# Cross network (DCN), six layers: pairs of row blocks taken in turn on shared weight tiles, a second product split into seven

## Chip, cores and metric

One NeuronCore of a Trainium2 chip runs the kernel. The metric is device time in microseconds (us), as the median of repeated runs. TensorE multiplies, VectorE adds and multiplies element by element, ScalarE moves results out of PSUM, and the queue of SyncE (SP) issues nearly all DMAs.

## What is computed

```python
# x0: 16384 x 1024, ws: 6 x 1024 x 1024, bs: 6 x 1024, all bf16
x = x0
for l in range(6):
    proj = x @ ws[l] + bs[l]
    x = x0 * proj + x
return x
```

## The kernel before

**Tiles.** The 16384 rows are cut into 16 pairs of row blocks, 2 x 512 rows each (`NPAIR`, L36). A pair lies transposed in SBUF: feature on the partition, row on the free axis. `x0T` holds the inputs of a pair and `xst` the running x, each [128, 2 blocks, 8 feature chunks, 512 rows].

**Seven products for eight.** A layer of a pair is a 2 x 2 block product: two halves of the features in, two halves out, two row blocks. L326 to L439 compute it with seven products of 512 x 512 weights by 512 rows instead of eight (a Strassen scheme). The products are numbered: 1, 2 and 4 use plain quarters of the weights, 5, 6, 3 and 7 use sums and differences of quarters ("combos", `emit_combo`, L120), which are made during the first pair and saved to DRAM (`Lc`). On the other side they need differences of x: T1 to T4 (`Ops.t`, L153). One product is 4 output chunks `m` of 4 matmuls each (`mm`, L279), every matmul 128x128 weights by 128x512, so seven products are 112 matmuls.

**Product 2 is split once more.** From the second pair on (`small`, L260) product 2 is itself done by seven products of 256 x 256 weights by 256 rows (`inner`, L286, 4 matmuls of 128x256 each, 28 in place of 16 of 128x512). Its differences of x are `ti` (`inner_t`, L160, four VectorE instructions of 128x512), its weight combos are "product 8". Its parts go out through ScalarE to EA and EB (`evi`, L298) and are added by VectorE (L374, L376).

**Sums.** Products 1, 6, 7 and 4 add up in the four banks `pA` one after another, and ScalarE reads them out (`ev`, L292) after each: P1s, then U2s (1+6), U3s (1+6+7), and the output sum with 4. Products 5 and then 3 share the banks `pX`: P5s and S53. VectorE forms the four output quarters C1 and C2 from these, multiplies by `x0T` (`f_mul`, L311) and adds to x (`f_add`, L314).

**Order.** The loops are pair (L227), then layer (L257). A step is one layer of one pair; there are 96. A layer needs the whole layer before it, so the T differences for the next layer stand at the end of the step (L444 to L452) between the last sums. VectorE and ScalarE instructions are pinned to program order (`vtt`, `acopy`, `abias`). PSUM has two pools of four banks that change roles at each step (L263).

**Loads.** Weight tiles (512 KB) go through a ring of 12 (`wring`, L60) on the SP queue, about ten tiles ahead (`prefetch_upto`, L89, `PREF` L85), in the order of all_keys: every pair loads all eight tiles of every layer again. The x0 of the next pair comes by DMA transposes during layer 0 (L473 to L479) into one of two `x0T` tiles. A finished pair is transposed by DMA from `xst` into its own `x0T` tile, which serves as scratch, and two DMAs write that out (L483 to L488). The last pair is written out differently, in part by TensorE transposes (`out_pe`, L242).

Of the kernel before, what the change touches and what calls it, by code (L numbers as in the profile page):

```python
# [8 lines left out]
ADD = mybir.AluOpType.add  # L9
# [8 lines left out]
def kernel(  # L18
# [19 lines left out]

    pin = tc.keep_in_program_order

    def vtt(out, in0, in1, op):
        return pin(nc.vector.tensor_tensor(out=out, in0=in0, in1=in1, op=op))  # L42

# [6 lines left out]
    NQ = NB // 2  # L50
    HE = H // 2

    const = ctx.enter_context(tc.tile_pool(name="const", bufs=1))
    dram = ctx.enter_context(tc.tile_pool(name="dram", bufs=1, space=bass.MemoryType.DRAM))
    x0t_pool = ctx.enter_context(tc.tile_pool(name="x0t", bufs=2))
    xst_pool = ctx.enter_context(tc.tile_pool(name="xst", bufs=2))
    t_pool = ctx.enter_context(tc.tile_pool(name="tp", bufs=1))
    ev_pool = ctx.enter_context(tc.tile_pool(name="evp", bufs=7))
    cb_pool = ctx.enter_context(tc.tile_pool(name="cbp", bufs=2))
    wring = ctx.enter_context(tc.tile_pool(name="wring", bufs=12))  # L60
    ti_pool = ctx.enter_context(tc.tile_pool(name="tip", bufs=1))
    ei_pool = ctx.enter_context(tc.tile_pool(name="eip", bufs=1))
    ps = [ctx.enter_context(tc.tile_pool(name=f"ps{i}", bufs=KH, space=bass.MemoryType.PSUM)) for i in range(2)]
    stage_ctx = ExitStack()
    w12_pool = stage_ctx.enter_context(tc.tile_pool(name="w12", bufs=2))
    xo_pool = None

    Lc = dram.tile([L, 5, P, KH * H], BF16, name="Lc")
    CIDX = {5: 0, 6: 1, 7: 2, 3: 3, 8: 4}

    def w_src(l, pid):
        wl = ws[l]
        if pid == 1:
            return wl[0:H, 0:H].rearrange("(k p) e -> p k e", p=P)
        if pid == 2:
            return wl[H:D, 0:H].rearrange("(k p) e -> p k e", p=P)
        if pid == 4:
            return wl[H:D, H:D].rearrange("(k p) e -> p k e", p=P)
        return Lc[l, CIDX[pid]].rearrange("p (k e) -> p k e", k=KH)

    ORDER = [1, 2, 8, 5, 3, 6, 7, 4]
    all_keys = [(pr, l, pid) for pr in range(NPAIR) for l in range(L) for pid in ORDER if pr > 0 or pid != 8]
    key_pos = {k_: i for i, k_ in enumerate(all_keys)}
    is_dma = lambda k_: not (k_[0] == 0 and k_[2] in CIDX)
    PREF = 10  # L85
    wtiles = {}
    state = {"next": 0}

    def prefetch_upto(n):  # L89
        while state["next"] < min(n, len(all_keys)):  # L90
            k_ = all_keys[state["next"]]
            if is_dma(k_) and k_ not in wtiles:
                wt = wring.tile([P, KH, H], BF16, name="wp")
                state["last_dma"] = nc.sync.dma_start(wt[:], w_src(k_[1], k_[2]))
                wtiles[k_] = wt
            state["next"] += 1
# [6 lines left out]
    combo_st = {}  # L103
    pending_saves = []

    def flush_saves():
        for (l_, pid_, t_) in pending_saves:
            si = nc.sync.dma_start(Lc[l_, CIDX[pid_]].rearrange("p (k e) -> p k e", k=KH), t_[:])
            if state.get("last_dma") is not None:
                nosync(si, state["last_dma"], "combo save behind the urgent weight loads")  # L110
        pending_saves.clear()

    def load_w12(l):
        st = combo_st.setdefault(l, {})
        if "w12" not in st:
            st["w12"] = w12_pool.tile([P, KH, H], BF16, name="w12")
            state["last_dma"] = nc.sync.dma_start(st["w12"][:], ws[l][0:H, H:D].rearrange("(k p) e -> p k e", p=P))
        return st["w12"]

    def emit_combo(l, pid):  # L120
        prefetch_upto(key_pos[(0, l, 4)] + 1)
        W11, W21, W22 = wtiles[(0, l, 1)], wtiles[(0, l, 2)], wtiles[(0, l, 4)]
        w12 = load_w12(l)
        t_ = wring.tile([P, KH, H], BF16, name="wp")
        if pid == 5:
            vtt(t_[:], w12[:], W22[:], ADD)
        elif pid == 6:
            vtt(t_[:], wtiles[(0, l, 5)][:], W11[:], SUB)
        elif pid == 3:
            vtt(t_[:], W21[:], wtiles[(0, l, 6)][:], SUB)  # L130
        elif pid == 8:
            i11, i12 = W21[:, 0:2, 0:HE], W21[:, 0:2, HE:H]
            i21, i22 = W21[:, 2:4, 0:HE], W21[:, 2:4, HE:H]
            iv = t_[:].rearrange("p k (j e) -> p k j e", e=HE)
            vtt(iv[:, 0], i12, i22, ADD)
            vtt(iv[:, 3], i11, i12, SUB)
            vtt(iv[:, 1], iv[:, 0], i11, SUB)
            vtt(iv[:, 2], i21, iv[:, 1], SUB)
        else:
            vtt(t_[:], W11[:], w12[:], SUB)  # L140
        if pid != 8:
            wtiles[(0, l, pid)] = t_
        pending_saves.append((l, pid, t_))

    class Ops:
        def __init__(self, x, flip, small):
            b = lambda dh, r: x[:, r ^ flip, dh * KH:(dh + 1) * KH, :]
            self.B = {(dh, r): b(dh, r) for dh in range(2) for r in range(2)}
            self.T = {}
            self.small = small  # L150
            self.ti = None

        def t(self, i):  # L153
            B, T = self.B, self.T
            T[i] = t_pool.tile([P, KH, NB], BF16, name=f"T{i}")
            in0, in1 = {1: lambda: (B[0, 1], B[0, 0]), 2: lambda: (B[1, 1], T[1][:]),
                        3: lambda: (B[1, 1], B[0, 1]), 4: lambda: (B[1, 0], T[2][:])}[i]()
            vtt(T[i][:], in0, in1, SUB)

        def inner_t(self, which):  # L160
            if not self.small:
                return
            if self.ti is None:
                self.ti = ti_pool.tile([P, 4, 2, NQ], BF16, name="ti")
            ti, b = self.ti, self.B[1, 0]
            b11, b12 = b[:, 0:2, 0:NQ], b[:, 0:2, NQ:NB]
            b21, b22 = b[:, 2:4, 0:NQ], b[:, 2:4, NQ:NB]
            for i in which:
                in0, in1 = {1: (b12, b11), 2: (b22, ti[:, 0]), 3: (b22, b12), 4: (b21, ti[:, 1])}[i]
                vtt(ti[:, i - 1], in0, in1, SUB)  # L170

        def rhs(self, pid):
            B, T = self.B, self.T
            return {1: B[0, 0], 2: B[1, 0], 3: B[1, 1]}[pid] if pid <= 3 else T[{4: 4, 5: 1, 6: 2, 7: 3}[pid]][:]

    LK = L * KD
# [6 lines left out]
    x0T_next = x0t_pool.tile([P, 2, KD, NB], BF16, name="x0T")  # L183
    xrows = [ev_pool.tile([P, KH, NB], BF16, name="ev") for _ in range(2)]
    xrows += [t_pool.tile([P, KH, NB], BF16, name=f"T{i}") for i in (3, 4)]
    raw = {i: wring.tile([P, KH, H], BF16, name="wp") for i in (1, 2, 4)}
    combo_st[0] = {"w12": w12_pool.tile([P, KH, H], BF16, name="w12")}
# [5 lines left out]
    pin(nc.scalar.dma_start(raw[1][:], w_src(0, 1)))  # L193
    pin(nc.scalar.dma_start(raw[2][:], w_src(0, 2)))
    pin(nc.scalar.dma_start(combo_st[0]["w12"][:], ws[0][0:H, H:D].rearrange("(k p) e -> p k e", p=P)))
    pin(nc.scalar.dma_start(raw[4][:], w_src(0, 4)))
    for i in raw:
        wtiles[(0, 0, i)] = raw[i]
    warm_in = const.tile([P, 1], BF16, name="warm_in")
    acopy(warm_in[:], zero[:, 0:1])  # L200
    warm = ps[1].tile([P, NB], FP32, name="px")
# [3 lines left out]
    def transpose_rows(q):  # L205
        n, h = q // 2, q % 2
        for k in range(KH):
            pt = ps[1].tile([P, NB], FP32, name="px")
            for r in range(KH):
                nc.tensor.matmul(pt[:, r * P:(r + 1) * P], lhsT=xrows[q][:, r, k * P:(k + 1) * P], rhs=ident[:],  # L210
                                 start=(r == 0), stop=True, skip_group_check=True)
            dst = x0T_next[:, n, h * KH + k, :]
            if k % 2 == 0:
                acopy(dst, pt[:])
            else:
                pin(nc.vector.tensor_copy(out=dst, in_=pt[:]))  # L216

    transpose_rows(0)
    pb = ps[1].tile([P, NB], FP32, name="px")
    nc.tensor.matmul(pb[:, 0:LK], lhsT=b_rows[:], rhs=ident[0:LK, 0:LK], start=True, stop=True)  # L220
    pin(nc.vector.tensor_copy(out=b_all[:], in_=pb[:, 0:LK]))
    prefetch_upto(7)
    ops = Ops(x0T_next, 0, False)
    prefetch_upto(PREF)

    step = 0
    for pr in range(NPAIR):  # L227
        x0T = x0T_next
        xst = xst_pool.tile([P, 2, KD, NB], BF16, name="xst")
        last_pair = pr == NPAIR - 1  # L230
# [11 lines left out]
        def out_pe(pts, n, ms, src, start, yo):  # L242
            for j in range(KH):
# [3 lines left out]
                if yo is None:  # L247
                    continue
# [270 lines left out]
```

## Time and profile before

| | us |
|---|---|
| median of 3 runs (2316.15 to 2316.91) | 2316.63 |
| profiled execution: its own time | 2314.74 |
| profiled execution: span from the first to the last instruction | 2313.0 |
| TensorE busy | 2287.3 |
| VectorE busy | 1994.0 |
| ScalarE busy | 1832.8 |

Granted TensorE clock: 1.000 of full speed. In the profile, PE is TensorE matmul, PEld its weight load, DVE is VectorE, ACT is ScalarE, SPq is SyncE's queue. A busy time of PE counts pipelined matmuls by modelled ends, so that the start of one matmul to the start of the next says more than the length of one. L42 is the helper `vtt`, through which all VectorE sums go, so there tiles tell the instructions apart. The DVE timeline gives the length of an instruction, too; where instructions follow each other without an idle note in brackets, the distance between two starts is what one really costs. Some matmul records are missing from the trace, so counts in a group can be low.

### The profile page before, as it was taken

How to read it: one execution, taken by the hardware profiler on the slowest of the kernel's cores; microseconds unless marked ns; L12 is line 12 of the kernel's file. 1: busy time of each engine (PE TensorE's matmuls, PEld its weight loads, DVE VectorE, ACT ScalarE, POOL GpSimd, SP SyncE). 2: the span in 40 equal slices, each digit the busy share in tenths (PEclk: the TensorE clock that was granted, in tenths of full speed). 3: DMA queues.
4: the chain of work that ended last, by engine and by line, in shares of the span. 5: the costliest groups of instructions: out<-in, count | busy, mean ns of one | idle time of the engine just before them, and what ended most of it. 6: DMA issues, size and time to landing. Idle time of an engine off the chain costs nothing.

```text
span 2313.0 us, 31780 instructions
## 1 busy us (share of the span) xinstructions
PE 2287.3 (99%) x11723; PEld 1163.4 (50%) x11953; DVE 1994.0 (86%) x2233; ACT 1832.8 (79%) x2974; POOL 0.7 (0%) x6
## 2 busy tenths in 40 slices
PE   8999999999999999999999999999999999999998
PEld 4444555545455554555555454555545555554544
DVE  7998888888888888888888888888888888888887
ACT  6777878878787887878788787878878787887877
POOL 0000000000000000000000000000000000000000
PEclk9999999999999999999999999999999999999999
DMA  7769586695966959668596685967859578595763
GB/s 237 245 212 289 173 219 245 183 281 174 230 234 185 279 183 232 227 189 272 183 240 224 193 267 180 255 209 194 270 173 271 195 196 267 172 294 174 211 217 106
DMA packets 603548, 507.53 MB, mean 219 GB/s; under 512 B 387329, under 2 KB 541953, under 8 KB 603393
## 3 DMA queue, kind: packets, MB, share of 16 engines
q1 hardware_dynamic: 601280, 503.39, 72.1%
q10 hardware_dynamic: 2112, 2.10, 0.3%
q8 instruction: 95, 1.56, 0.3%
q14 instruction: 61, 0.49, 0.1%
HBM read 392.18 MB, written 49.28 MB: 191 GB/s over the span
## 4 chain that ended last, share of the span: by engine, by line
PE 92%; DVE 5%; issue 1%; DMA 0%; ACT 0%; DVEq 0%; ACTq 0%
PE px L283 80%; PE px L289 12%; DVE cb L42 2%; DVE wp L42 1%; DVE xst L42 1%; DVE T L42 1%; DMA ev<-in_x_dram 0%; ACT ev L45 0%; DMA wp<-in_ws_dram 0%; DMA Lc<-wp 0%; DVE x0T L216 0%; PE px L210 0%; DVE ti L42 0%; ACT cb L48 0%; ACT ev L48 0%
## 5 line engine op out<-in xcount | busy, mean ns | idle before, releaser
L283 PEld LDWEIGHTS <-wp 128*128 128x128 bf16 x9312 | 909.7, 98 | 1010.3 <-issue 7.1
L283 PE MATMUL px<-T,wp 128*128 128x512 bf16 x5992 | 1393.2, 379 | 10.2 <-DVE wp L42 2.1
L48 ACT ACTIVATE ev<-px,b_all 128x512 bf16<-128x512 f32 x1152 | 791.6, 687 | 224.2 <-PE px L283 216.2
L283 PE MATMUL px<-xst,wp 128*128 128x512 bf16 x2575 | 615.1, 379 | 6.5 <-DVE xst L42 3.1
L45 ACT CAST ev<-px 128x512 bf16<-128x512 f32 x798 | 466.5, 585 | 179.5 <-PE px L283 166.3
L42 DVE TENSOR_TENSOR cb<-cb,x0T 128x2048 bf16<-128x2048 bf16 (+1 forms) x386 | 469.8, 1218 | 9.9
L42 DVE TENSOR_TENSOR cb<-ev 128x1024 bf16<-128x1024 bf16 (+1 forms) x390 | 263.0, 696 | 231.4 <-ACT ev L45 231.4
L42 DVE TENSOR_TENSOR xst<-cb,xst 128x2048 bf16<-128x2048 bf16 x319 | 390.8, 1225 | 23.1 <-DVE cb L42 0.9
L48 ACT ACTIVATE cb<-px,b_all 128x512 bf16<-128x512 f32 x384 | 263.8, 687 | 67.7 <-PE px L283 55.6
L289 PEld LDWEIGHTS <-wp 128*128 128x128 bf16 x2520 | 246.0, 98 | 127.1
L289 PE MATMUL px<-ti,wp 128*128 128x256 bf16 x1440 | 215.8, 272 | 0.0
L45 ACT CAST ea<-px 128x512 bf16<-128x512 f32 x360 | 211.8, 588 | 0.0
L42 DVE TENSOR_TENSOR T<-xst,T 128x2048 bf16<-128x2048 bf16 x160 | 195.5, 1222 | 9.0 <-PE px L289 0.9
L42 DVE TENSOR_TENSOR T<-xst 128x2048 bf16<-128x2048 bf16 x160 | 194.9, 1218 | 0.0
L45 ACT CAST eb<-px 128x512 bf16<-128x512 f32 x270 | 160.2, 593 | 0.0
L289 PE MATMUL px<-xst,wp 128*128 128x256 bf16 x900 | 135.0, 273 | 0.0
L283 PE MATMUL px<-x0T,wp 128*128 128x512 bf16 x515 | 122.8, 379 | 0.8
L42 DVE TENSOR_TENSOR ea<-ea,eb 128x1024 bf16<-128x1024 bf16 (+1 forms) x180 | 99.9, 555 | 20.4 <-ACT eb L45 20.4
L42 DVE TENSOR_TENSOR cb<-ev,ea 128x2048 bf16<-128x2048 bf16 x90 | 109.7, 1218 | 0.0
L42 DVE TENSOR_TENSOR xst<-cb,x0T 128x2048 bf16<-128x2048 bf16 x64 | 78.4, 1225 | 2.2
L42 DVE TENSOR_TENSOR ti<-xst 128x512 bf16<-128x512 bf16 x150 | 63.2, 422 | 3.6
L42 DVE TENSOR_TENSOR ti<-xst,ti 128x512 bf16<-128x512 bf16 x150 | 62.7, 418 | 0.0
(33 smaller groups left out, 201.1 us busy)
## 6 DMA issues: line engine op xcount, KB each, us to landing
wp<-Lc SPq DMA_DIRECT2D x450, 512.0 KB, 3.7
wp<-in_ws_dram SPq DMA_DIRECT2D x285, 512.0 KB, 4.3
out_dram<-x0T SPq DMA_DIRECT2D x30, 1024.0 KB, 10.0
Lc<-wp SPq DMA_DIRECT2D x30, 512.0 KB, 3.1
w<-in_ws_dram SPq DMA_DIRECT2D x5, 512.0 KB, 4.5
wp<-in_ws_dram ACTq DMA_DIRECT2D x3, 512.0 KB, 7.6
ev<-in_x_dram SPq DMA_DIRECT2D x2, 512.0 KB, 6.9
T<-in_x_dram SPq DMA_DIRECT2D x2, 512.0 KB, 10.3
```

The lines of the kernel that those rows point to most:

```text
L42: return pin(nc.vector.tensor_tensor(out=out, in0=in0, in1=in1, op=op))
L45: return pin(nc.scalar.copy(out=out, in_=in_))
L48: return pin(nc.scalar.activation(out=out, in_=in_, func=IDENT, bias=bias, scale=1.0))
L283: nc.tensor.matmul(pts[m][:], lhsT=wt[:, k, m * P:(m + 1) * P], rhs=rhs[:, k, :], start=(start and k == 0), stop=(k == KH - 1), **kw)
L289: nc.tensor.matmul(pt[:, m * NQ:(m + 1) * NQ], lhsT=w[:, k, m * P:(m + 1) * P], rhs=rhs[:, k, :], start=(start and m == 0 and k == 0), sto ...
```

## The change

The changed kernel runs two pairs, A and B, side by side: for each of 8 couples `s`, for each layer, first the step of A and then the step of B, with the same weight tiles. The weights are loaded once per couple and layer: 7 x 6 x 9 = 378 loads after the first couple, through a ring of 11. Nothing is prefetched in A's step but what is missing; in B's step each product requests the tile ten places further on.

Product 4 is split like product 2, in all steps of couples 1 to 7 but the very last (83 steps), with its own differences `ti4` and its own weight combos ("product 9"). Product 2 is split in all 84 steps of couples 1 to 7; the first couple (pairs 0 and 1, 12 steps) splits nothing, while in the kernel before pair 1 split product 2. Of product 4's seven parts four go out through ScalarE into e4 and e5, three add into `pA` directly.

What a step leaves over is done at the start of the next step, which belongs to the other pair (`trail`, `defer`): the last of the seven parts of product 4, two of its read-outs, and the four VectorE steps of C2 (sum, correction by e4 and e5, multiplication, addition). The T differences move to the start of the pair's own step. T1 and T3 become one VectorE instruction of 128x4096 (T13), and so do the multiplications and the additions of C2's two halves. The half sums of 128x1024 become whole ones of 128x2048.

A finished pair is stored in the other pair's step (`store_out`). There are three `x0T` tiles; B's x0 is loaded during A's layer 0, one step ahead of its use. At the end, the last pair is written out wholly through TensorE transposes, 80 matmuls in five groups with 16 read-outs (`rows_out`).

The core of the diff, the new lines only where the old ones are gone as a whole:

```diff
-    x0t_pool = ctx.enter_context(tc.tile_pool(name="x0t", bufs=2))
-    ev_pool = ctx.enter_context(tc.tile_pool(name="evp", bufs=7))
-    wring = ctx.enter_context(tc.tile_pool(name="wring", bufs=12))
+    x0t_pool, xst_pool = pool("x0t", 3), pool("xst", 2)
+    ev_pool, cb_pool, wring = pool("evp", 6), pool("cbp", 2), pool("wring", RING)
-    ORDER = [1, 2, 8, 5, 3, 6, 7, 4]
+    ORDER = [1, 2, 8, 5, 3, 6, 4, 9, 7]
+            if part is None:
+                vtt(self.t13[:], self.src[:, 1].rearrange("p (i k) b -> p i k b", i=2), self.src[:, :, 0:KH, :], SUB)
+    def trail(Y, prompt):
...
+        out = [lambda: vtt(C2[:, 1], Y.U3s[:], Y.P5s[:], ADD)]
+        if Y.E4 is not None:
+            def s4():
+                e = Y.E4
+                for i in range(2):
+                    vtt(e[:, 2 * i:2 * i + 2, NQ:NB], e[:, 2 * i:2 * i + 2, (1 - i) * NQ:(2 - i) * NQ], Y.e5[:], ADD)
+            out.append(s4)
+            out.append(lambda: vtt(C2[:, 0], C2[:, 0], Y.E4[:], ADD))
+        out.append(lambda: vtt(C2[:], C2[:], eh1(x0T), MULT))
+        out.append(lambda: vtt(eh1(dst), C2[:], eh1(src), ADD))
-    for pr in range(NPAIR):
-        for l in range(L):
+    for s in range(NPAIR // 2):
+        for l in range(L):
+            for side in ("A", "B"):
+                X, Y = cur[side], prev
+                in2, in4 = s > 0, s > 0 and not last
...
+                todo = trail(Y, False)
+                if not first:
+                    X.T13()
...
+                mm(1, w1, pA, 0, True)
+                if Y is not None and Y.defer is not None:
+                    Y.defer()
+                ev(P1s, pA, 0, 0)
+                prompt = Y is not None and Y.l == L - 1
...
+                    own = [X.T2, X.T4]
+                    if in4:
+                        own.append(lambda: setattr(X, "ti4", inner_t(X.T[4], "ti4")))
+                seq = todo + own if prompt else [f for pair in zip(todo + [None] * 9, own + [None] * 9) for f in pair if f is not None]
+                for f in seq:
+                    f()
+                if prompt:
+                    store_out(Y)
...
+                if need2 and not late:
+                    N.ti2 = inner_t(N.rhs(2), "ti2")
...
+                fin(C1, 0, 0)()
...
+                if in4:
+                    mm(6, w6, pA, 0, False)
+                    ev(U2s, pA, 0)
+                    inner(half(z1), wr4[0, 0], b4[0, 0], True)
+                    evi(e4[0, 0], z1)
+                    mm(6, w6, pA, 1, False)
+                    ev(U2s, pA, 1)
+                    inner(half(z5), wj[:, 0], t4[:, 0], True)
+                    evi(X.e5[:], z5)
+                    mm(6, w6, pA, 2, False)
+                    ev(U2s, pA, 2)
+                    inner(half(z1), wj[:, 1], t4[:, 1], False)
+                    evi(e4[0, 1], z1)
+                    mm(6, w6, pA, 3, False)
+                    ev(U2s, pA, 3)
+                    mm(7, w7, pA, 0, False)
+                    ev(U3s, pA, 0, 1)
+                    inner(half(z1), wj[:, 3], t4[:, 2], False)
+                    evi(e4[1, 0], z1)
+                    for m in range(1, KH):
+                        mm(7, w7, pA, m, False)
+                        ev(U3s, pA, m, 1)
+                    inner(col(0, 0), wr4[1, 0], b4[1, 0], False)
+                    inner(col(0, 1), wj[:, 2], b4[1, 1], False)
+                    for m in range(2):
+                        ev(C2[:, 0], pA, m, 1)
+                    def defer(pA=pA, C2=C2, wr4=wr4, t4=t4, ev=ev, inner=inner, col=col):
+                        inner(col(2, 0), wr4[1, 1], t4[:, 3], False)
+                        for m in range(2, KH):
+                            ev(C2[:, 0], pA, m, 1)
...
+                vtt(C1[:, 1], U2s[:], S53[:], ADD)
+                fin(C1, 0, 1)()
```

## Prediction

> **What bounds the kernel now.** I read the page's busy times first, then the chain of work that ended last, then the timelines of single engines in one steady step (700 to 724 us). The page:
>
> ```profile
> PE 2287.3 (99%) x11723; PEld 1163.4 (50%) x11953; DVE 1994.0 (86%) x2233; ACT 1832.8 (79%) x2974; POOL 0.7 (0%) x6
> PE 92%; DVE 5%; issue 1%; DMA 0%; ACT 0%; DVEq 0%; ACTq 0%
> ```
>
> TensorE is the bound; VectorE has some 3 us in 24 to spare; no DMA is on the chain. So time is won only by fewer matmul columns, and only while VectorE keeps up. Now TensorE's timeline, steady step:
>
> ```profile
> 713.18 1.03 PE L283 MATMUL px<-xst,wp 128*128 128x512 bf16 x4
> 714.04 0.60 PE L289 MATMUL px<-xst,wp 128*128 128x256 bf16 x4
> 714.48 1.03 PE L283 MATMUL px<-T,wp 128*128 128x512 bf16 x4
> 715.34 0.60 PE L289 MATMUL px<-ti,wp 128*128 128x256 bf16 x4
> 715.78 0.60 PE L289 MATMUL px<-xst,wp 128*128 128x256 bf16 x4
> 716.21 1.03 PE L283 MATMUL px<-T,wp 128*128 128x512 bf16 x4
> ```
>
> Compare starts: four wide matmuls (128x512) take 0.86 us, four narrow ones (128x256) 0.435. The longest pieces of the chain repeat every 118.99 us, five steps (338.23, 457.22): a step is 23.80 us. It has 24 groups of four wide and 7 of four narrow, so a wide group is (23.80 - 7 x 0.435)/24 = 0.865. VectorE's timeline of the same step:
>
> ```profile
> 711.01 1.22 DVE L42 TENSOR_TENSOR T<-xst 128x2048 bf16<-128x2048 bf16 x1
> 712.14 0.42 DVE L42 TENSOR_TENSOR ti<-xst,ti 128x512 bf16<-128x512 bf16 x1
> 712.48 0.42 DVE L42 TENSOR_TENSOR ti<-xst 128x512 bf16<-128x512 bf16 x1
> 712.81 0.42 DVE L42 TENSOR_TENSOR ti<-xst,ti 128x512 bf16<-128x512 bf16 x1
> 713.15 1.22 DVE L42 TENSOR_TENSOR cb<-cb,x0T 128x2048 bf16<-128x2048 bf16 x1
> 714.40 1.22 DVE L42 TENSOR_TENSOR xst<-cb,xst 128x2048 bf16<-128x2048 bf16 x1
> 715.73 1.23 DVE L42 TENSOR_TENSOR T<-xst,T 128x2048 bf16<-128x2048 bf16 x1
> ```
>
> Starts lie closer than durations: 128x2048 costs 1.135 us when the next instruction doesn't need its result (711.01 to 712.14), 1.25 to 1.33 when it does (713.15, 714.40), 128x512 costs 0.335. The same timeline gives 0.605 for 128x1024. In pair 0, where VectorE also makes the weight combos, its queue is full and the step is 24.69 us (its Lc saves start at 48.78, 73.47, 98.14); these prices add up to 24.6 there. I trust them.
>
> **TensorE.** A step with both splits has 20 wide and 14 narrow groups: 20 x 0.865 + 14 x 0.435 = 23.39 us, against 23.80: 0.41 less. Before, pairs 2 to 15 are 84 steps of 23.80 = 1999.2; after, 83 of 23.39 and the last of 23.80 = 1965.2: **-34.0**.
>
> **First couple.** Before, pair 1 starts at 161.8 us and ends six steps later at 304.6. After: 12 steps without a split, 28 wide groups = 24.22 each by TensorE. VectorE there needs some 21 us (a layer's combos now fall on two steps, and three pairs of instructions are merged), so TensorE sets 24.2. The first step ran from 6.91 to 37.45, with 2.2 of waiting for VectorE's combos, which now come earlier; say 35.5. But the second step belongs to B, whose T13 stands in VectorE's queue behind the combos of layer 1, and these need weights queued on SP behind four x0 transposes (about 5 us each to issue) and four saves. That puts the weights near 36 and T13's end near 46, while TensorE wants it at 35.5 + 2 x 3.46 = 42.4: 3 us of wait. 35.5 + 3 + 11 x 24.22 = 304.9: **0** (bounds -3, no wait, and +6).
>
> **VectorE, one steady step after.** The built program has 22 instructions a step. Three of 128x4096 (T13, C2's multiplication and addition), by extrapolation 1.135 + 2048 x (1.135 - 0.335)/1536 = 2.20 each, one with a dependent next: 6.75. Ten of 128x2048: four dependent at 1.25 to 1.29, six at 1.135: 11.8. EA + EB 0.605 + 0.43, e4's correction 0.67, ti2 and ti4 1.47 each (as the four combos at 48.67). Sum **23.2**. No row shows a 128x4096; two whole durations of 128x2048 would be 2.45, and the floor is the slope alone, 2.13. Without any dependency cost the sum is 22.3; with every instruction at its whole duration (1.22, 0.42, 0.69, 2.29) it is 24.4. I take 23.2, nearest to the rows and to pair 0. So VectorE has 0.2 us to spare in 23.39. Waits in it: C1's second sum needs U2s, whose last read-out I lay at 19.45 us (16 wide, 11 narrow groups, 0.8 for ScalarE); VectorE comes there at 19.2. T13 may start when product 7 of the step before has read the old one, 0.87 before that step ends. It ends near 2.0; product 5 reads it at 5.2 (4 wide and 4 narrow groups). So VectorE can be 3 us late before TensorE feels it. If VectorE needs over 23.39, the step follows it one for one: 84 us per us.
>
> A rule speaks against the change. The Trainium skill, page "VectorE: DVE Perf Modes", section "The DRAIN you can't avoid", has the next instruction start only when the pipe of the one before is empty. Then each would cost its duration, and by that the step would be about 24.4 and the kernel slower; the starts above, 1.13 apart at durations of 1.22, contradict it.
>
> **ScalarE.** Now 16 read-outs with bias, at 0.59 from start to start (714.24 to 714.83), and 19 without, at 0.48 (716.02 to 716.50): 18.6 of 23.4 us. It hides. Each narrow product finds its bank read out over 0.8 us before, but for product 2's, which now waits 0.03 (717.51 to 718.40) and will again: 0.
>
> **Loads.** Half the weight traffic goes, but the list of waits names no weight load before a steady matmul: 0. A's step issues hardly any load and B's step nine, as tiles come free, each at least 5 us before use.
>
> **Ends of couples.** SP's queue at the end of a pair before:
>
> ```profile
> 1310.48 10.55 SPq L484 DMA_TRANSPOSE x0T<-xst  x1
> 1321.13 1.00 SPq L94 DMA_DIRECT2D wp<-Lc  x2
> 1322.41 6.20 SPq L487 DMA_DIRECT2D out_dram<-x0T  x2
> 1328.71 5.08 SPq L94 DMA_DIRECT2D wp<-in_ws_dram  x2
> 1335.04 11.57 SPq L477 DMA_TRANSPOSE x0T<-in_x_dram  x2
> ```
>
> From the store's transpose to the x0 load is 24.6 us, and its second half lands some 13 us later (5.8 to issue the first, 7.4 to landing by the page). After, the store of A starts about 9.8 us into B's last step, so B's new x0 lands at 47 to 49 with four weight loads in the queue; B's first step starts at 46.8 and its T13 would start at about 48 and is needed at 52. Just in time; the product before it needs only the first half. Seven such places, 0 to 3 us each: **+3**. The new `xst` is first written 5 us after the old one's transpose has landed.
>
> **End.** Before, 8.8 us from the last product (2304.2) to the end. After, ten read-outs on ScalarE follow the last product instead of six, one after the other, about 7.4 us, then the last write (2.9 to landing, 1.3 to the end): 11.6. Also pair 14's store (24.5 us from its transpose to landed writes, begun 9.8 into the last step of 23.8) is still writing at +10.5, ahead of the last writes: 13.5. **+4.7** (2.8 to 7).
>
> **Sum.** 2313.0 - 34.0 + 0 + 3 + 4.7 = 2286.7 span. The profiled execution's own time is 1.7 above its span, and the median of the runs 1.9 above that: **2290**.
>
> **Rivals.**
> - VectorE slightly over (128x4096 at 2.3 to 2.4, or new dependency gaps): step 23.5 to 23.7, on average +0.2 x 84 = 17: 2307. For: the margin is 1%. Against: pair 0's sum fits to 0.1. Chance 0.17.
> - **Slower:** VectorE's instructions can't overlap as before, because nearly every one now waits for another engine or the one before, so each costs its whole duration: step 24.4, +1.05 x 84 = +88: 2378. It decides from 23.70 (26 us/84 over 23.39). For: the duration column; against: the starts. Chance 0.10, with its milder forms from 2321.
> - B's x0 comes late at the seven couple ends: another 5 us each would put T13 3 us too late, 7 x 3 = 21: 2311. For: SP's long issue times in a row; against: 4 us of reserve. Chance 0.07.
> - The change doesn't bring fewer columns at full pace: narrow products alternate with wide ones on two banks, and each of e4's three returns to bank z1 waits for ScalarE. Price half the gain, 0.2 x 84 = 17: 2307. Against: a wide group lies between. Chance 0.05.
>
> **How the numbers follow.** Likeliest, TensorE-bound at 23.4, 2290, own range 2281 to 2299: 0.61. Range 2280 to 2313: it takes in the milder rivals and the bounds of the start and end, and leaves out the slow one. Within 0.2% (4.6 us, about what a measurement can tell) is 2312 to 2321. Faster 0.84, same 0.05, slower 0.11.
>
> **What would show it.** Right: steady steps 23.4 apart, PE near 99%, DVE busy about 96% with a short wait for ScalarE before C1's second sum, 128x4096 starts 2.2 apart. Wrong: PE idle before product 5 or 6 put down to DVE (T13, T2), DVE without any idle time and steps over 23.5, PE idle before B's first layers put down to DMA, more than 15 us after the last wide product.

## The result, and the profile after

The changed kernel takes 2303.63 us (median of 4 runs, 2302.99 to 2307.08) against 2316.6 before on the same chip: ratio 0.9947, 95% interval 0.993 to 0.9964. It is faster, by 13 us where 26 were forecast. Its profiled execution took 2303.93 us, span 2302.1; the forecast span was 2286.7, so 15.4 us are missing there. (In the median 13.6 are missing, since it lies 0.3 us below the profiled execution's own time, where the forecast added 1.9.) The page's busy times and the shares of the chain, as shown of before:

```profile
PE 2259.3 (98%) x12658; PEld 1258.0 (55%) x12909; DVE 2186.7 (95%) x2328; ACT 1912.4 (83%) x3294; POOL 0.7 (0%) x6
PE 81%; DVE 7%; DMA 7%; SPq 2%; issue 1%; ACT 0%; DVEq 0%
```

VectorE is now nearly as busy as TensorE (86% before), and DMAs, which had 0% of the chain, and SP's queue, which did not appear in it, have 9%. Where the time lies is read from three landmarks of TensorE's timeline: the first matmul of A's first step of couple 1 (before: of pair 2's first step), the first transposing matmul after the last product, and the end (us):

| | first couple | couples 1 to 7 | end | span |
|---|---|---|---|---|
| before | 305.1 | 1999.1 | 8.8 | 2313.0 |
| predicted | 304.9 | 1968.2 | 13.5 | 2286.7 |
| after | 312.2 | 1972.0 | 17.8 | 2302.1 |

So 7.3 of the missing 15.4 us lie in the first couple, 3.8 in the couples, 4.3 at the end.

**The steady step is as forecast.** Three steps take 70.14 us (the chain's longest pieces stand at 368.24, 438.38 and 508.52): 23.38 each, forecast 23.39. Such a stretch in numbers (columns: window, its length, busy us and count of PE, PEld, DVE, ACT, POOL, granted clock, DMA share, GB/s):

```profile
368.24:438.38 70.14, 69.72 (x402) 39.92 (x408) 69.21 (x77) 60.00 (x105) 0.00 (x0) 1.00 0.41 107
```

VectorE's timeline where it lags behind TensorE and so runs at its own pace:

```profile
1017.82 2.29 DVE L46 TENSOR_TENSOR T<-xst 128x4096 bf16<-128x4096 bf16 x1
1020.02 1.22 DVE L46 TENSOR_TENSOR cb<-ev 128x2048 bf16<-128x2048 bf16 x1
...
1041.01 2.28 DVE L46 TENSOR_TENSOR T<-xst 128x4096 bf16<-128x4096 bf16 x1
```

T13 costs 2.20 from start to start, with a duration of 2.28, and one step of VectorE's work is 1041.01 - 1017.82 = 23.19 us. Both were forecast (2.20 and 23.2).

**The start.** TensorE, whose notes in brackets tell idle time and releaser, and SP's queue at the first step of B and the next step of A:

```profile
51.65 5.18 PE L295 MATMUL px<-T,eb 128*128 128x512 bf16 x16 [7.63 <-DVE T L46]
56.67 1.67 PE L295 MATMUL px<-x0T,wp 128*128 128x512 bf16 x7
```

```profile
6.35 19.53 SPq L198 DMA_TRANSPOSE x0T<-in_x_dram  x3
...
27.03 5.68 SPq L198 DMA_TRANSPOSE x0T<-in_x_dram  x1
...
34.85 2.72 SPq L112 DMA_DIRECT2D wp<-in_ws_dram  x3
```

Product 5 waits 7.63 us for its T, which stands in VectorE's queue behind the combos of layer 1, which wait for raw weights that SP issues from 33.9 us on. Before them stand four x0 transpositions, two of them for pair 2, whose x0 VectorE first reads at 297.29. After the pause the 16 matmuls of product 5 took 5.02 us (51.65 to 56.67) where a product takes 3.45. The stretches of the profile tell why (columns as above):

```profile
52.00:57.00 5.00, 5.00 (x18) 2.04 (x17) 5.00 (x4) 1.88 (x4) 0.00 (x0) 0.72 0.00 0
57.00:62.00 5.00, 5.00 (x25) 2.25 (x23) 4.93 (x5) 3.79 (x6) 0.00 (x0) 1.00 0.01 2
```

The granted clock is 0.72 over the 5 us after the pause and 1.00 after that. The Trainium skill, page "TensorE: Matmul & The Clock Gate", section "What's actually happening", says that an idle window of some 3.4 us halves the clock and a busy one of that length restores it. By that a pause costs about 1.7 us more (an estimate from that page); here it was 5.02 - 3.45 = 1.57, which agrees.

**A couple's end.** SP, VectorE and TensorE around the end of a couple, B's last step starting at 1132.81:

```profile
1143.88 9.63 SPq L250 DMA_TRANSPOSE x0T<-xst  x1
...
1168.07 11.70 SPq L198 DMA_TRANSPOSE x0T<-in_x_dram  x2
```

```profile
1141.56 2.29 DVE L46 TENSOR_TENSOR xst<-cb,xst 128x4096 bf16<-128x4096 bf16 x1
...
1183.43 2.29 DVE L46 TENSOR_TENSOR T<-x0T 128x4096 bf16<-128x4096 bf16 x1 [1.65 <-DMA x0T<-in_x_dram]
```

```profile
1185.78 1.04 PE L295 MATMUL px<-T,wp 128*128 128x512 bf16 x4 [0.84 <-DVE T L46]
```

A's rows are finished at 1143.85, 11.0 us into the step (forecast 9.8); SP needs 39.5 us from there to B's x0; T13 starts 50.6 us after B's last step began (forecast 48), and product 5 waits. At couple 1's end that step begins at 568.96 and the rows are ready at 578.75, 9.8 us into it as forecast; T13, with 2.02 us of waiting for x0, still starts only at 619.02, 50.1 us into it. The six ends between couple 1 and couple 7 cost 7.7 us together (1972.0 less the 1964.3 that e9 below takes without a wait); the seventh such place, where the first couple ends at 312, shows no wait.

**The end.** SP's last issues:

```profile
2270.93 9.67 SPq L250 DMA_TRANSPOSE x0T<-xst  x1
2283.35 5.00 SPq L254 DMA_DIRECT2D out_dram<-x0T  x2
2288.43 9.98 SPq L534 DMA_DIRECT2D out_dram<-ev  x8
```

The last product ends at 2284.26. Pair 14's output writes are issued around then, and the eight last writes stand behind them until 2298.4.

### The profile page after: what moved, and what is told of

Its sections match the earlier page's. It is cut to its first block, busy times and chain, and to the rows that moved or that the text cites. A ratio compares the mean times of both kernels' runs of the same rounds, so it can differ in the third digit from the quotient of the medians.

```text
span 2302.1 us, 33220 instructions
## 1 busy us (share of the span) xinstructions
PE 2259.3 (98%) x12658; PEld 1258.0 (55%) x12909; DVE 2186.7 (95%) x2328; ACT 1912.4 (83%) x3294; POOL 0.7 (0%) x6
## 4 chain that ended last, share of the span: by engine, by line
PE 81%; DVE 7%; DMA 7%; SPq 2%; issue 1%; ACT 0%; DVEq 0%
PE px L295 63%; PE px L301 18%; DMA x0T<-xst 3%; DVE cb L46 3%; DMA out_dram<-x0T 3%; SPq L198 2%; DVE T L46 2%; DMA x0T<-in_x_dram 2%; DVE xst L46 1%; DVE ti L46 1%; DMA wp<-in_ws_dram 0%; DVE ea L46 0%; PE px L527 0%; SPq L254 0%; DVE e L46 0%
## 5 line engine op out<-in xcount | busy, mean ns | idle before, releaser
L295 PEld LDWEIGHTS <-wp 128*128 128x128 bf16 x7888 | 771.2, 98 | 742.1 <-DVE T L46 6.5
L295 PE MATMUL px<-T,wp 128*128 128x512 bf16 x4499 | 1111.6, 379 | 11.4 <-DVE T L46 4.8
L301 PEld LDWEIGHTS <-wp 128*128 128x128 bf16 x4676 | 457.2, 98 | 250.2 <-DMA wp<-in_ws_dram 1.6
L46 DVE TENSOR_TENSOR cb<-cb,x0T 128x2048 bf16<-128x2048 bf16 (+2 forms) x291 | 454.4, 1562 | 4.6
L301 PE MATMUL px<-ti,wp 128*128 128x256 bf16 x2672 | 400.9, 273 | 0.0
L46 DVE TENSOR_TENSOR xst<-cb,xst 128x2048 bf16<-128x2048 bf16 (+1 forms) x240 | 378.2, 1576 | 9.2 <-PE px L527 0.5
L46 DVE TENSOR_TENSOR cb<-ev 128x2048 bf16<-128x2048 bf16 (+1 forms) x205 | 248.8, 1214 | 30.5 <-ACT ev L52 30.1
L52 ACT CAST e<-px 128x512 bf16<-128x512 f32 x332 | 195.3, 588 | 0.7 <-PE px L301 0.7
L46 DVE TENSOR_TENSOR T<-xst 128x4096 bf16<-128x4096 bf16 x80 | 182.7, 2284 | 0.0
L301 PE MATMUL px<-T,wp 128*128 128x256 bf16 x996 | 135.9, 273 | 0.7 <-DMA wp<-in_ws_dram 0.7
L46 DVE TENSOR_TENSOR cb<-ev,ea 128x2048 bf16<-128x2048 bf16 x84 | 102.9, 1225 | 11.1 <-ACT ev L55 2.6
L46 DVE TENSOR_TENSOR cb<-cb,e 128x2048 bf16<-128x2048 bf16 x83 | 101.2, 1220 | 1.3
```

Source lines behind the costliest of these rows:

```text
L52: return pin(nc.scalar.copy(out=out, in_=in_))
L295: nc.tensor.matmul(pts[m][:], lhsT=wt[:, k, m * P:(m + 1) * P], rhs=rhs[:, k, :], start=(start and k == 0), stop=(k == KH - 1), **kw)
L301: nc.tensor.matmul(dst(m), lhsT=w[:, k, m * P:(m + 1) * P], rhs=rhs[:, k, :], start=(start and m == 0 and k == 0), stop=(k == 1), skip_gro ...
```

## The experiments

Theory **Q**: the steps are as forecast, and the rest is lost in SP's queue, which sets the start, the couples' ends and the end. Rival **V**: VectorE's full queue makes these waits, whatever SP does. All times are us; the landmarks are those of the table above. "Time" is the median of the runs (of e3 and e6, one run).

| kernel | first couple | couples 1 to 7 | end | span | time |
|---|---|---|---|---|---|
| after | 312.2 | 1972.0 | 17.8 | 2302.1 | 2303.63 |
| e1_x0_behind_raw | 302.9 | 1973.4 | 17.6 | 2293.9 | 2294.12 |
| e2_store_halves | 315.1 | 1979.4 | 15.8 | 2310.3 | 2312.22 |
| e3_no_store_transpose | 320.5 | 1964.3 | 16.9 | 2301.7 | 2303.48 |
| e6_no_store14 | 313.6 | 1976.0 | 11.2 | 2300.8 | 2302.56 |
| e7_raw_lasthalf | 302.9 | 1972.5 | 16.5 | 2291.9 | 2293.72 |
| e8_outs_pool | 303.1 | 2136.5 | 16.7 | 2456.3 | 2459.95 |
| e4_no_split4 | 314.0 | 1997.2 | 13.8 | 2325.0 | 2328.36 |
| e5_dve_plus1 | 313.8 | 2000.3 | 19.4 | 2333.5 | 2337.51 |
| e5_dve_plus2 | 313.6 | 2035.6 | 19.3 | 2368.4 | 2371.46 |
| e9_raw_no_store_transpose | 304.3 | 1964.3 | 15.0 | 2283.6 | 2284.43 |
| e10_tail_writes_act | 303.9 | 1973.4 | 15.9 | 2293.1 | 2294.66 |
| e11_no_split4_last_layer | 304.3 | 1969.5 | 11.0 | 2284.8 | 2286.28 |

**e1: raw weights of layer 1 ahead of pair 2's x0.**

```diff
-            pin(eng.dma_start(t[:], raw_src(l, pid)))
+            ld = pin(eng.dma_start(t[:], raw_src(l, pid)))
+            if eng is nc.sync:
+                state["last_dma"] = ld
```

`load_x0` already holds its transpositions behind the DMA in `state["last_dma"]`; the edit sets it during the first couple, too.

> The x0 transposes of pair 2 (two, some 6 us of SP issue each) no longer stand among the first DMAs; they are queued behind the weight loads of layer 2. Theory Q (SP's queue): in the changed kernel the weights of layer 1 are issued at 33.9 to 37.6 us, because two x0 transposes of pair 2 stand before them; without these they go out at about 27, VectorE's combos for layer 1 start at about 33 instead of 41.6, T13 ends before TensorE asks for it at 43.9, and the 7.6 us wait in the second step falls below 1 us: 7 us less, about 2296.5. Theory V (VectorE's queue itself is too full there, 36 us of work in the first 60): the wait stays above 5 us and the time at 2303 to 2304.

Ratio to before 0.9911 (0.9897 to 0.9924). SP now issues the raw weights 9 us earlier, behind two transpositions instead of four:

```profile
25.17 1.18 SPq L112 DMA_DIRECT2D ea<-in_ws_dram  x1
26.41 2.67 SPq L112 DMA_DIRECT2D wp<-in_ws_dram  x3
```

The wait before product 5 is gone and the first couple ends 9.3 us sooner, 7.6 of waiting and 1.6 of lowered clock. SP's order alone did this: Q for the start.

**e2: every store's transposition in two halves.**

```diff
-        nc.sync.dma_start_transpose(out=xo, in_=Y.xst[:].rearrange("r n k b -> r (n k b)"))
+        for n in range(2):
+            nc.sync.dma_start_transpose(out=Y.x0T[:, n].rearrange("p k (j r) -> p (k j) r", r=P),
+                                        in_=Y.xst[:, n].rearrange("r k b -> r (k b)"))
```

> The store of a finished pair transposes its two row blocks by two DMAs instead of one, so that the first write can start while the second half is still in flight. Theory Q: the writes are issued when SP is done with the second transpose, some 2 us earlier than now; the x0 of B, which waits for them, lands 2 us earlier, and the waits at the six later ends of couples (7.7 us in all, 0.5 to 2.5 each) fall to 2 or less; the end after the last product falls from 17.8 to about 15.5. Together 7 to 8 us less: about 2296. Theory V (the ends of couples wait because VectorE, with 0.2 us to spare in a step, comes late by itself): ends of couples stay at 7 to 8 us, at most the end gains, 2301 to 2304.

A miss: 0.9987 (0.9978 to 0.9996) of before. The end fell as expected (15.8), but the built program now puts the output writes ahead of two weight loads, and TensorE waits 1.6 to 3.1 us for product 3's weights at each couple's end, 13.0 us at the six; the start's wait was 9.66 us. An edit to one DMA had moved its neighbours in the queue.

**e3: no transposition in the A pairs' stores up to pair 12**, so that these output rows aren't the reference's.

```diff
-        nc.sync.dma_start_transpose(out=xo, in_=Y.xst[:].rearrange("r n k b -> r (n k b)"))
+        if Y.pr % 2 == 1 or Y.pr == NPAIR - 2:
+            nc.sync.dma_start_transpose(out=xo, in_=Y.xst[:].rearrange("r n k b -> r (n k b)"))
```

> The DMA transposes of the stores of pairs 0, 2, ... 12 are left out, so that the rows of these pairs receive what x0T holds and not x; all else is as in the changed kernel. Theory Q: B's x0 can be loaded 12 us earlier, and the waits at the ends of couples vanish (7.7 us to under 1), the steady step stays 23.38: one profiled execution at about 2296 to 2297. Theory V: the waits stay, 2303 to 2304.

The couples' ends lost all their waits (1964.3, 7.7 less), but an output write, now free of the transposition, slipped ahead of the raw weights, and the start's wait grew to 15.1 us: the total is unchanged. e9 repeats it without that.

**e6: pair 14's store left out**, so that its rows aren't written.

```diff
-                if prompt:
+                if prompt and not last:
```

> The store of pair 14, which falls into the last step, is left out: its rows are not written. Theory Q: the end after the last product (17.8 us) is long because the last eight writes stand behind this store on SP and in the DMA engines; without it 11 to 12 us, so 6 us less: about 2298. Rival (the ten read-outs one after the other and the TensorE transposes make it): the end stays at 16 us or more.

The end is 11.2 us, 6.6 less. The store, not the last pair's own work, made the difference to 17.8. The total hardly fell, as in this one run the start and the couples took 5.4 us more, which the edit doesn't explain.

**e7: e1's edit, and the last store alone in halves**

```diff
-        nc.sync.dma_start_transpose(out=xo, in_=Y.xst[:].rearrange("r n k b -> r (n k b)"))
+        if Y.pr == NPAIR - 2:
+            for n in range(2):
+                nc.sync.dma_start_transpose(out=Y.x0T[:, n].rearrange("p k (j r) -> p (k j) r", r=P),
+                                            in_=Y.xst[:, n].rearrange("r k b -> r (k b)"))
+        else:
+            nc.sync.dma_start_transpose(out=xo, in_=Y.xst[:].rearrange("r n k b -> r (n k b)"))
```

> Edit: layer 1's raw weights are no longer overtaken on SP by the second pair's x0 transpositions (as in e1_x0_behind_raw), and the last staged store, that of pair 14, is transposed in two halves; the other stores stay whole, so that SP's order at the couple ends is that of the changed kernel. Theory Q (SP's order sets the start, the couple ends and the end): the start as in e1 (9.5 us less than the changed kernel's 2303.6), couple ends as there (about 7 us of waits stay), and the end 15.8 us instead of 17.6, as in e2_store_halves: 2303.6 - 9.5 - 1.8 = 2292.3. Theory V (VectorE's full queue makes the waits): SP's time at the end is not what it waits for, and the time stays that of e1, 2294.1.

Ratio 0.9907 (0.9895 to 0.992), 2293.72 us: between the two forecasts, which lie too close together for the time to decide. The end gained 1.1 us of the 1.8. In the stretch 52 to 57 us the clock is now 1.00, without a pause ahead of it (after: 0.72):

```profile
52.00:57.00 5.00, 5.00 (x25) 2.25 (x23) 4.93 (x8) 3.59 (x6) 0.00 (x0) 1.00 0.17 67
```

**e8: e7, and the stores' output writes on GpSimd's queue.**

```diff
-                nc.sync.dma_start(out[r0:r0 + NB, :].rearrange("(j p) (k r) -> p k j r", p=P, r=P),
+                nc.gpsimd.dma_start(out[r0:r0 + NB, :].rearrange("(j p) (k r) -> p k j r", p=P, r=P),
```

> Edit: e7_raw_lasthalf with the staged stores' output writes issued by GpSimd's queue instead of SP's. GpSimd is otherwise idle. Theory Q: at a couple end SP spends 5.9 us less before it issues the next B pair's x0, so x0's second half lands some 5 us earlier than in the changed kernel, where it came 2 to 4 us late: the waits of TensorE at the couple ends fall from 7 us in all to 2 or less, and the last writes at the end, which stand behind 5.0 us of output writes on SP, are issued up to 5 us earlier: 2292.3 - 5 - 3 = about 2284, and no more than 2289. Theory V: the waits at the couple ends stay, and the time is within 2 us of e7. A third outcome: GpSimd makes its own descriptors, and if that takes something from VectorE, whose time decides, the time rises instead.

The worst miss: 1.0621 (1.0597 to 1.0645). GpSimd's and SP's queues at one couple's end:

```profile
890.05 5.04 POOL L261 DMA_DIRECT2D out_dram<-x0T  x2 [273.35 <-DMA x0T<-xst]
```

```profile
899.74 15.75 SPq L257 DMA_TRANSPOSE x0T<-xst  x1
915.59 19.16 SPq L200 DMA_TRANSPOSE x0T<-in_x_dram  x2
```

The next x0 goes into the tile that A's writes read (the first row). These two landed 14.1 us after their issue (8.9 in e7), and the built program put x0 behind B's transposition, which waits for VectorE's last sum of B: x0 is issued 40 us after A's transposition began (875.84), where e7, with x0 ahead of B's transposition, has 25 (852.57 to 877.81). TensorE waits 21 to 25 us at each end. VectorE's instructions elsewhere cost what they did before (T13 2.20 from start to start), so it is not a load on VectorE. Most of it is x0's place in the queue; how much the slower writes add, this run doesn't separate.

**e4: product 4 not split at all.**

```diff
-                in2, in4 = s > 0, s > 0 and not last
+                in2, in4 = s > 0, False
```

> Edit: the two pairs still run in turn, but product 4 goes back to four wide groups in every step (product 2 stays split); so TensorE's step is 24 wide groups of 0.865 us and 7 narrow of 0.435, 23.80 us instead of 23.39, and VectorE loses the four subtractions of the split and the additions behind it. If TensorE's groups set the step, as the prediction had it: 83 steps x 0.41 = 34 us more, 2338 us, less up to 5 us of waits at the couple ends that VectorE's new slack takes away: 2332 to 2338, slower than the kernel before (2316) with its single pair. If VectorE's full queue set the step instead, its lighter load would pay part of the 34 back: under 2325.

1.0054 (1.0041 to 1.0067): slower than before; 2328.36 lies between the two forecasts, 4 us below the first one's band. The step is 23.78 us (forecast 23.80) and every couple 285.32. So TensorE's groups set the step. What was missed: not one wait of TensorE is left at the couples' ends, and the end took 13.8 us, though SP's queue holds the same DMAs. With 4 us of spare time in a step VectorE finishes the stored rows 5.9 us into it (11.0 after), so SP starts that much sooner. So Q, which left VectorE out, falls; call the mended theory **V'**: a chain from VectorE's last sum through SP's 40 us to x0 (or to the last writes).

**e5: one or two more 128x512 subtractions per steady step on VectorE** (repeats of the first one of `ti2`; `3` in e5_dve_plus2).

```diff
-        vtt(ti[:, 0], b[0, 1], b[0, 0], SUB)
+        for _ in range(2 if name == "ti2" else 1):
+            vtt(ti[:, 0], b[0, 1], b[0, 0], SUB)
```

> Edit: the first 128x512 subtraction of the operands of product 2 is done three times instead of once, so VectorE has two more such instructions per steady step; nothing else reads them. The prediction had VectorE at 23.2 us of work in a step of 23.39. From the trace of the changed kernel one more costs about 0.335 us, so 23.19 + 2 x 0.335 = 23.86 us of work: VectorE sets the step, which is 0.47 us longer, 83 x 0.47 = 39 us: 2343 us. If VectorE had more slack than its busy time shows (0.7 us or more in a step), the time stays at 2303.6.

> Edit: as e5_dve_plus2, with one repeated 128x512 subtraction per steady step instead of two. In e5_dve_plus2 each repetition moved VectorE's next start by 0.46 us (a repeat waits for the end of the one before, as both write the same place), and the step was 24.11 us = 23.19 + 2 x 0.46. So here VectorE's work is 23.65 us against TensorE's 23.38: the first 0.19 us of the 0.46 is VectorE's spare time and free, the other 0.27 us is paid in each of 83 steps: 22 us, and 1 to 6 us more at the couple ends, where VectorE then finishes the stored rows later: 2327 us (2324 to 2332). If VectorE had no spare time at all, 83 x 0.46 = 38 us: 2342 us; if it had more than 0.46 us, 2304.

Both miss in size, 1.024 (1.0225 to 1.0255) and 1.009 (1.0075 to 1.0105), but the step answers exactly. VectorE's timeline in e5_dve_plus1:

```profile
1046.00 1.22 DVE L46 TENSOR_TENSOR ti<-xst 128x512 bf16<-128x512 bf16 x3
...
1077.62 2.28 DVE L46 TENSOR_TENSOR T<-xst 128x4096 bf16<-128x4096 bf16 x1
...
1101.27 2.28 DVE L46 TENSOR_TENSOR T<-xst 128x4096 bf16<-128x4096 bf16 x1
```

The next instruction starts 1.13 us after these three, 0.67 after the two of the changed kernel: a repeat into the same place costs 0.46, not 0.335. The step is 1101.27 - 1077.62 = 23.65 with one and 24.11 with two, that is 23.19 + 0.46 n. So VectorE's spare time was 0.19 us in a step (forecast 0.2), and beyond it the step follows one for one. With one repeat the steps account for 83 x 0.27 = 22 us; the rest of its 31 us of span lies at the couples' ends (6), the start and the end (1.6 each).

**e9: e3 on top of e7, with the output writes held in their place** (the same rows aren't the reference's).

```diff
-        else:
+        elif Y.pr % 2 == 1:
             nc.sync.dma_start_transpose(out=xo, in_=Y.xst[:].rearrange("r n k b -> r (n k b)"))
...
+                nosync(o, state["last_dma"], "behind the weight loads already issued")
```

> Edit: e7_raw_lasthalf, and the A pairs 0 to 12 are stored without the transposition (their output rows aren't those of the reference; the writes stay and are held behind the weight loads already issued). SP is 10 us less busy ahead of the next B pair's x0. Theory Q: the 5.8 us of waits at the couple ends in e7_raw_lasthalf are gone, and the rest stays: 2293.7 - 5.8 = 2288 us. Theory V (VectorE's backlog alone makes these waits): 2293.7 stays. The steps, the start and the end should stay as in e7_raw_lasthalf in both.

0.9862 (0.9847 to 0.9877), 2284.43 us where Q had 2288: the couples gave back 8.2 us, not 5.8, and the end 1.5. Each couple takes 280.56 us = 12 x 23.38, with no wait at any end. Taking away SP's part of the chain is enough, as Q said. And with no wait VectorE has no lag: A's rows are finished 9.8 us into B's last step, as forecast (11.1 in e7).

**e10: e7 with four of the eight last writes on ScalarE's queue.**

```diff
-                nc.sync.dma_start(out[r0:r0 + 2 * P, ...
+                (nc.scalar if n == 1 else nc.sync).dma_start(out[r0:r0 + 2 * P, ...
```

> Edit: e7_raw_lasthalf, and of the eight last output writes the four of the second row block are issued by ScalarE's queue instead of SP's. In e7_raw_lasthalf SP issues the eight from 2277.86 on, 1.26 us each, to 2287.98, while the last rows are ready at 2282.5. Theory Q (SP's issuing sets the end): SP ends its four at 2282.9 or just behind the last rows, and the end comes 3 to 4 us earlier: 2290 us. If the last write's own landing sets the end, or ScalarE's evictions are held up by issuing as long as SP was: 2293.7, or 1 to 2 us more.

A miss: 0.9905 (0.989 to 0.9919), as e7. SP took 8.75 us for four writes (10.12 for eight in e7), and they landed after 5.6 us instead of 3.2. So the number of writes on SP doesn't make the time. Where pair 14's 2 MB are not on their way at that moment, SP issues the eight in 5.7 us (e6) or 5.8 (e11 below): what costs is the store beside them. How it slows the issue, no run shows.

**e11: e7 with product 4 unsplit in each couple's last layer only.**

```diff
-                in2, in4 = s > 0, s > 0 and not last
+                in2, in4 = s > 0, s > 0 and l < L - 1
```

> Edit: e7_raw_lasthalf, with product 4 as four wide groups in the two steps of each couple's last layer only, where the stored rows are finished. Each such step costs TensorE 0.40 us more (23.78 instead of 23.38, as e4_no_split4 showed): 13 steps, 5.2 us. VectorE has some 4 us less work in each of them. Theory V' (formed from e4_no_split4: VectorE finishes the stored rows 11.0 us into the step where e4 has them at 5.9, and SP's chain of transposition, writes and x0, some 41 us long, starts from there): the rows are ready about 4 us earlier, the 5.8 us at the couple ends go, and so do 2 to 3 us of the 16.5 at the end: 2293.7 + 5.2 - 5.8 - 2.7 = 2290.4 us. If SP's queue alone decides (Q without VectorE's part): only the 5.2 are added, 2299 us.

0.9868 (0.9852 to 0.9885): at 2286.28 us the fastest kernel that writes all rows, although TensorE has 5.2 us more to do. V' had 2290.4; the end gave 5.5 us where 2 to 3 were expected. Its chain, then SP and VectorE at the couple's end whose last step of B starts at 1124.62:

```profile
PE 99%; DMA 1%; DVE 0%; ACTq 0%; ACT 0%; DVEq 0%; issue 0%
```

```profile
1130.48 10.38 SPq L257 DMA_TRANSPOSE x0T<-xst  x1
...
1156.01 12.94 SPq L200 DMA_TRANSPOSE x0T<-in_x_dram  x2
```

```profile
1128.17 2.29 DVE L46 TENSOR_TENSOR xst<-cb,xst 128x4096 bf16<-128x4096 bf16 x1
...
1172.52 2.29 DVE L46 TENSOR_TENSOR T<-x0T 128x4096 bf16<-128x4096 bf16 x1
```

The rows are ready 5.8 us into the step (11.0 after), T13 starts without a wait 47.9 us after it began, and every couple takes 281.35 us = 12 x 23.38 + 2 x 0.40. The end, SP's last issues:

```profile
2255.90 9.69 SPq L254 DMA_TRANSPOSE x0T<-xst  x2
2265.69 4.93 SPq L261 DMA_DIRECT2D out_dram<-x0T  x2
2275.69 5.79 SPq L541 DMA_DIRECT2D out_dram<-ev  x8
```

Pair 14's writes are issued 8 us before the last product ends (2273.81), and the end takes 11.0 us, as without the store (e6).

## Why the forecast was right in kind and twice too large

- **TensorE's step, -34.0: right.** 23.38 measured; without any wait couples 1 to 7 take 1964.3 (e9), forecast 1965.2.
- **VectorE's 23.2 in 23.39: right**, by the row (T13's 2.20) and by the added instructions (e5). The slower rival, whole durations, did not come: starts lie 2.20 apart at durations of 2.28. The section of the Trainium skill that the prediction sets against this (page "VectorE: DVE Perf Modes", "The DRAIN you can't avoid") was read by half: the same paragraph adds that an instruction that isn't held back starts earlier, so these starts don't contradict the page.
- **First couple, 0 (bounds -3 to +6): the step that failed most**, +7.1 (312.2 against 305.1; the prediction's 304.6 for before is 0.5 too low). The order of SP's queue was seen, the time it takes was not. The four x0 transpositions held SP for 25.2 us (19.53 + 5.68), not for about 20; the raw weights "near 36" were issued from 33.9 to 37.6 and reached VectorE up to 44.5; T13 ended at 51.6, not near 46. So TensorE's wait was 7.6 us and not 3. The pause then brought the lowered clock, 1.6 us, which the sum did not have, and the first step ended at 36.95, not at 35.5. With SP's order mended the term is -2.2 (e1) to -0.8 (e9, e11), inside its bounds. The wait also differed between profiled executions of kernels that share this start (6.6 to 9.7 in after, e2, e4, e5 and e6); why, and why the transpositions took SP longer than 5 us each, stays open.
- **Couple ends, +3: mis-sized**, 7.7, at six places. SP gave x0 later than the 47 to 49 forecast: at couple 1's end the rows were ready at 9.8, as the sum has it, and T13 still started at 50.1. From there on the rows are late, too (11.0 at the end shown): the sum left out that VectorE, once late, wins back only 0.19 us per step, some 2 us in a couple. The "4 us of reserve" set T13's start (48) against the time by which its result is needed (52); with T13's own 2.2 us it was under 2. The rival with x0 late had the right place; its price of 21 was too high. Either half of the chain, mended alone, removes TensorE's waits (e9, e11).
- **End, +4.7 (2.8 to 7): mis-sized**, +9.0, out of its bounds. Pair 14's rows came 10.9 us into the last step, not 9.8, and the eight last writes took SP 10.0 us beside pair 14's output, until 14.2 us after the last product, where the sum had the whole end at 13.5. The term for the last pair's own work, 11.6, was right: without the store beside it the end is 11.0 to 11.2 (e11, e6). What was mis-sized is the store, 6.6 us.
- The terms that failed all hang on work that TensorE's steady groups don't show: three short stretches, 16 us of error, against a steady part that was right to 1 us. By its time alone the result could pass for the rival at 2307 (VectorE slightly over); steps of 23.38 rule that out.

## To carry to other kernels

A resource with 1% to spare costs nothing in the steady state and still shows wherever something starts from its last result: follow the chain from there through the queue to its next user, with the lag that it cannot win back. Giving up a little of the gain where that chain starts (e11, 5.2 us on TensorE) can return more than it costs. When one DMA in a shared queue is edited, read the built order of its neighbours before trusting the price of the edit.

## What the runs showed that was not expected

- After a pause of 7.6 us TensorE's next 5 us ran at a granted clock of 0.72; in e8, after a pause of 15.8 us at a couple's end, at 0.53 over 5.1 us. That is some 2.4 us lost there (0.47 x 5.1), against 1.6 in the changed kernel, so the price of a pause isn't fixed, and the 1.7 estimated above is only near it.
- Output writes of 1 MB landed 16.4 us after their issue from GpSimd's queue (median of the 30 in e8) and 9.2 from SP's (e7), though the transpositions beside them lay differently as well.
- A VectorE instruction that writes where the one before it wrote costs 0.46 us for 128x512, against 0.335 without (e5).
- In the changed kernel one DMA transposition holds SP's queue for 3.9 to 10.2 us (512 rows of x0, median 5.3) or 9.6 to 10.4 (a whole pair); the loads behind it wait that long, as the raw weights of layer 1 did.
